# One closing If for the general path, in place of an If between two expert slots and a cascade behind the last

## Chip, cores and metric

The kernel runs on one core of one Trainium2 chip. The metric is the device time of one execution in microseconds (us), median over runs. The core has a matrix engine (TensorE, PE in the profile; its weight loads are PEld), VectorE (DVE), ScalarE (ACT), GpSimd (POOL) and SyncE (SP), which here issues most of the DMAs.

## What is computed

A gated linear attention over 4 x 8 heads, 768 steps, head size 48, then two mixture-of-experts layers (8 experts, one chosen per token, 384 -> 1024 -> 384 with a ReLU), the first with a capacity of 768 tokens per expert, the second with an output gate. There are 3072 tokens, all numbers are float32.

```python
f = 1.0 / (1.0 + np.exp(-f_logit))
for t in range(S):
    state = f[:, :, t, :, None] * state + np.einsum('bhd,bhe->bhde', k[:, :, t], v[:, :, t])
    y[:, :, t] = np.einsum('bhd,bhde->bhe', q[:, :, t], state)
# x: y as [3072, 384]; layer 1
expert_idx = np.argmax(x @ w_gate, axis=1)        # gate_w: its softmax weight
disp[e, counts[e]] = x[i]                         # the first `capacity` tokens of each expert
h = np.maximum(np.einsum('ecd,edf->ecf', disp, w1), 0.0)
y = np.einsum('ecf,efd->ecd', h, w2)
out[i] = gate_w[i] * y[expert_idx[i], pos[i]]     # 0 for a token beyond the capacity
# layer 2: the same with own weights, no capacity, and
out[mask] = gate_w[mask, None] * sigmoid(x @ w_output_gate)[mask, e, None] * ye
```

## The kernel before

**Stages.** `attention` works through 24 blocks of 128 steps; while it does so it routes the tokens of layer 1 (`tok_route`) and scatters their rows, sorted by expert, into a buffer `xs1` in HBM (POOL, L376). Small constants (`iota`, L141 to L157, `consts_late`, L189) are made on the way, one group per block. From about 147 us on the kernel works in *slots*: a slot reads a fixed number of rows of one expert from `xs1`, transposes them (`xt_jobs`, L497), splits them into a high and a low part (xh, xl) and runs both matrix products (`layers`, L1034) with three matmuls for each product: high by high, high by low, low by high. The weights are loaded by SP into `raw` (L218) and split by ACT and DVE (L231, L232) into one of two sets in turn.

**Order of the slots.** The expert with the most tokens is known before attention ends; the first slot, *early*, takes its first 256 rows. Then come the ranks 0 to 7 of layer 1, the experts in order of their counts; rank 0 is the early slot's expert again, with the rest of its rows (112 x 2 = 224) and the same weights. Layer 2 has the same: an early slot and nine slots more (`SLOTS2`). The shapes are fixed at compile time, from 224 to 432 rows.

**What fills the gaps.** `layers` calls `hook(f)` behind each of its eight first-layer tiles (f) and three second-layer tiles (m), and the hooks issue other work there: the routing of the slot before (`post1_jobs`, L1081: matmuls with the gate at L1094, then some 25 small DVE and ACT steps, among them rank matmuls on PE at L329, then scatters into `xs2`), the transposes for the next slot (L503), weight splits, gates. Each engine works through its own instructions in the order in which the program issues them (`manual_schedule`).

**SP's queue around the change.** Row reads (`read_rows`, L1012), zeroing DMAs behind a slot's rows (`rank_zeros` -> `zero_rows`, L210) and weight loads stand in one queue. Reads and zeroing of `xs1` follow one another through the data.

**The general path.** What the fixed slots don't hold is counted in `rare`: a flag of the attention (`fla`, some decay too small), rows beyond the room of the slots (`nover`), rows beyond the capacity (`drop`). For the inputs timed here all are 0 and no part of the general path runs. It stands at two places: between the early slot and rank 0, an If on `rare` (L1267, L1268) that may redo attention and routing and then go through a cascade of eleven nested Ifs (`cascade1`), one leftover slot each; and behind the last slot of layer 2, a second cascade (`cascade2`, L1368) on a count `nv2` (L1364). `plan2.overflow` (L948, 25 DVE operations, in the hooks of the first slot of layer 2) makes that count and the lists for the cascade.

A value is loaded for an If on each engine (`values_load`), and each engine branches by itself. Where the branch skips the body, a few semaphore updates behind it bring the semaphores to the state that the body would have left.

Of the kernel before, what the change touches and what calls it, by code (L numbers as in the profile page):

```python
# [9 lines left out]
F32 = mybir.dt.float32  # L10
F32R = mybir.dt.float32r
# [35 lines left out]
NOV = 11  # L47
# [16 lines left out]
def moe_attention_kernel(ctx: ExitStack, tc, blk, vblk, iw1, iw2, w1a, w2a, w1b, w2b, cap, out):  # L64
# [73 lines left out]

    iota_i = cp.tile([128, E * NOV], I32, name="iota_i")

    def iota(name, shape, pattern, base, cm):  # L141
        ti = iota_i[:, :shape[1]] if len(shape) == 2 else iota_i.rearrange("p (a b) -> p a b", a=shape[1])
# [728 lines left out]
    class Plan:  # L871


        def __init__(self, tag, slots, room, early):
# [10 lines left out]
            self.nf = t("o_nf", [128, 1])  # L885
            self.ni = t("o_ni", [1, 1], I32)
            self.thr = t("o_thr", [128, NOV])
            self.row0 = t("o_row0", [1, NOV], I32)
            self.wrow = t("o_wrow", [1, NOV], I32)
# [58 lines left out]
        def overflow(self):  # L948

            def t(n, shape):  # L950
                if n not in state:
                    state[n] = cp.tile(shape, F32, name=n)
                return state[n]

# [20 lines left out]
            def sm(out, x):  # L975
# [8 lines left out]
                lambda: V.tensor_copy(self.nf, cum[:, E - 1:E]),  # L984
                lambda: V.tensor_copy(self.ni, cum[0:1, E - 1:E]),
# [17 lines left out]
                tt(self.row0, nj[0:1], live[0:1], ALU.mult),  # L1003
                stt(self.wrow, ej[0:1], 128.0, live[0:1], ALU.mult, ALU.mult),
            ]
            return count, where
# [19 lines left out]
    def ovf_rows(xs, o, j):  # L1026
        s = slot(OV, o.thr[:, j:j + 1], xs)
        read_rows(s, xs, o.row0[0:1, j:j + 1])
        return s
# [4 lines left out]
    def layers(s, st, hook, rows_out=False, parts=False):  # L1034
        N = s.N
        hh, hl = ([hbuf[:, i * NM:i * NM + N] for i in range(o, o + KF)] for o in (0, KF))
# [154 lines left out]
    W += [lambda l, j=j: weights_at(plan2.wrow[0:1, j:j + 1], l, wb[l]) for j in range(NOV)]  # L1191
# [15 lines left out]
    wq = ctx.enter_context(tc.tile_pool(name="wq", bufs=1))  # L1207
    whl.append([[wq.tile([128, 3072], F32R, name=f"w{l}{hl}1") for hl in "hl"] for l in (1, 2)])
    hbuf = wq.tile([128, 2 * KF * NM], F32R, name="hbuf")
    wy = ExitStack()  # L1210
    ybuf = [wy.enter_context(tc.tile_pool(name="wy", bufs=1)).tile([128, 2 * KD * NM], F32R, name="ybuf")]

    def outputs(n, parts):

        if not parts and len(ybuf) == 1:
            wy.close()
            ybuf.append(ctx.enter_context(tc.tile_pool(name="wz", bufs=1)).tile([128, KD * NM], F32, name="yT"))
        b = ybuf[0] if parts else ybuf[1]
        return [b[:, i * KD * NM:i * KD * NM + KD * n].rearrange("p (k n) -> p k n", k=KD) for i in range(1 + parts)]
# [28 lines left out]

    def post1_now(s):
        run(gate_jobs(s) + sum(post1_jobs(s), []))  # L1250
        V.tensor_copy(base2, state["base"])
        state["base"] = base2

    def cascade1(j, nv):
        with tc.If(nv > j):
            for l in (0, 1):
                weights_at(plan1.wrow[0:1, j:j + 1], l, wa[l])
            s = ovf_rows(xs1, plan1, j)
            run(xt_jobs(s))
            run(split_jobs(1))  # L1260
            layers(s, 1, lambda i: None, parts=True)
            post1_now(s)
            if j + 1 < NOV:
                cascade1(j + 1, nv)

    at = turn[0]
    rv = nc.values_load(rare[0:1, 0:1], min_val=0, max_val=128 + 2 * E)  # L1267
    with tc.If(rv > 0):  # L1268
        fv = nc.values_load(fli[0:1, 0:1], min_val=0, max_val=128)
        with tc.If(fv > 0):  # L1270
            general_attention()
            reroute()
            state["base"] = base2
            V.memset(early1.offs, 0.0)
            V.memset(early1.thr, 0.0)
            V.tensor_copy(early1.ints[:, 4:5], early1.row[0:1])
            run(plan1.order(base1f, True))
        run(sum(plan1.overflow(), []))
        nc.sync.dma_start(out=out.rearrange("(p j) c -> p j c", j=NT // 128),
                          in_=zrow[:, :DM].unsqueeze(1).to_broadcast([128, NT // 128, DM]))  # L1280
        post1_now(cur)
        V.memset(early1.thr, 0.0)
        for e in range(E):
            zero_rows(xs1, plan1.tail[0:1, e:e + 1], NO)
        cascade1(0, nc.values_load(plan1.ni[0:1, 0:1], min_val=0, max_val=NOV))
        for l in (0, 1):
            W[1](l)
        run(halves(split(1, None, None))[0])
        read_rows(nxt, xs1, early1.ints[0:1, 4:5])
        run(xt_jobs(nxt))  # L1290

    turn[0] = at
# [145 lines left out]
```

## Time and profile before

| | us |
|---|---|
| median of 3 runs | 647.56 (647.36 to 654.54) |
| the profiled execution, its time | 645.49 |
| its span in the trace | 643.7 |
| PE busy | 608.9 (95%) |
| DVE busy | 409.5 (64%) |
| ACT busy | 320.8 (50%) |
| POOL busy | 159.5 (25%) |
| mean granted clock of PE | 0.98 |

The profile is of one execution; its times are those of the trace, counted from the start of the span. A busy share is the share of a stretch in which the engine worked on an instruction; branches, register loads, semaphore updates and the issue of DMAs are not counted as busy. Matmuls are pipelined: a matmul's duration is longer than the distance to the next one's start. The granted clock of PE is in parts of 2.4 GHz.

### The profile page before, as it was taken

Reading aid. Unit: us, or ns where it says so; the run is one execution under the profiler, and the core shown is the slowest. Engines: PE = TensorE matmul, PEld = TensorE weight load, DVE = VectorE, ACT = ScalarE, POOL = GpSimd, SP = SyncE. Lnnn points to the kernel's source line nnn. Section 1 sums busy time; section 2 is a strip of 40 time slices with the busy share of each in tenths; the row PEclk is TensorE's granted clock in tenths of the full one; section 3 lists DMA queues with packets and bytes.
Section 4 is the critical chain, followed back from the end, with each engine's and each line's share of the span. In section 5 each row is a group of like instructions: output and inputs, shape, how many; then the busy total and the mean of one; then the engine's idle time right before and its main releaser. Section 6 shows DMA issues by size and latency. Waiting matters only on the chain.

```text
span 643.7 us, 13335 instructions
## 1 busy us (share of the span) xinstructions
PE 608.9 (95%) x4888; PEld 588.3 (91%) x4888; DVE 409.5 (64%) x1119; ACT 320.8 (50%) x722; POOL 159.5 (25%) x223
## 2 busy tenths in 40 slices
PE   8999998897599999999999999999999999999991
PEld 7898887787599999999999999999999999999991
DVE  7888999978366656657585866618544544654620
ACT  3665654555244453636365463345554544764530
POOL 2567667646001102020202201110110111111120
PEclk9999998999979999999999999999999999999997
DMA  9987884957166446546475272086644435665300
GB/s 237 258 211 205 233 214 140 280 166 280 42 187 217 157 149 177 175 138 198 137 243 170 67 241 76 23 268 193 241 163 135 161 115 189 210 230 150 137 28 21
DMA packets 31540, 110.40 MB, mean 172 GB/s; under 512 B 4109, under 2 KB 15154, under 8 KB 27614
## 3 DMA queue, kind: packets, MB, share of 16 engines
q1 hardware_dynamic: 26158, 95.05, 48.4%
q0 software_dynamic: 5296, 14.30, 6.8%
q8 instruction: 42, 0.69, 0.5%
q14 instruction: 44, 0.36, 0.2%
HBM read 83.47 MB, written 26.21 MB: 170 GB/s over the span
## 4 chain that ended last, share of the span: by engine, by line
PE 40%; issue 26%; POOL 4%; ACT 0%; POOLq 0%
PE pys L1072 17%; PE phs L1044 12%; PE pxs L1044 6%; POOL out L376 4%; PE ptr L1094 1%; PE pys L1094 1%; PE phs L503 1%; PE pxs L503 0%; POOLq L376 0%; ACT w1h L231 0%; ACT hbuf L1046 0%; PE pmt L329 0%; PE pys L1143 0%; PE ptr L1143 0%; ACT yT L1078 0%
## 5 line engine op out<-in xcount | busy, mean ns | idle before, releaser
L1072 PE MATMUL pys<-hbuf,w2h 128*128 128x360 f32 (+10 forms) x864 | 206.8, 321 | 1.0 <-DVE hbuf L1047 1.0
L1072 PEld LDWEIGHTS pys<-hbuf,w2h 128*128 128x128 f32 x864 | 149.8, 188 | 2.5 <-DVE hbuf L1047 1.4
L1072 PE MATMUL pys<-hbuf,w2l 128*128 128x360 f32 (+10 forms) x432 | 137.8, 319 | 0.0
L1044 PE MATMUL phs<-xh,w1h 128*128 128x360 f32 (+10 forms) x306 | 100.9, 330 | 7.0 <-DVEq L1268 4.6
L376 POOL DMA_INDIRECT xs<-xrow,r_dest x53 | 54.9, 1036 | 201.7 <-ACT w2h L231 90.1
L1044 PE MATMUL phs<-xl,w1h 128*128 128x360 f32 (+10 forms) x306 | 98.0, 320 | 0.5 <-DVE xl L505 0.5
L1044 PE MATMUL phs<-xh,w1l 128*128 128x360 f32 (+10 forms) x306 | 97.8, 320 | 0.0
L232 DVE TENSOR_TENSOR w2l<-raw,w2h 128x512 fp32r<-128x512 f32 x96 | 65.5, 686 | 47.0 <-ACT w2h L231 46.5
L232 DVE TENSOR_TENSOR w1l<-raw,w1h 128x512 fp32r<-128x512 f32 x96 | 65.0, 689 | 28.1 <-ACT w1h L231 27.5
L1072 PEld LDWEIGHTS pys<-hbuf,w2l 128*128 128x128 f32 x432 | 81.5, 189 | 0.5
L376 POOL DMA_INDIRECT out<-xrow,oid x31 | 30.2, 975 | 183.8 <-ACT xrow L1144 174.6
L1047 DVE SCALAR_TENSOR_TENSOR hbuf<-phs,hbuf 128x360 fp32r<-128x360 f32 (+10 forms) x102 | 50.9, 499 | 30.8 <-ACT hbuf L1046 30.5
L1046 ACT ACTIVATE hbuf<-phs 128x360 fp32r<-128x360 f32 (+10 forms) x102 | 46.1, 451 | 40.9 <-PE phs L1044 38.8
L1044 PEld LDWEIGHTS phs<-xh,w1h 128*128 128x128 f32 x306 | 58.9, 193 | 7.8 <-issue 4.8
L231 ACT CAST w2h<-raw 128x512 fp32r<-128x512 f32 x96 | 59.2, 622 | 1.3 <-DMA raw<-w2b 1.3
L1044 PEld LDWEIGHTS phs<-xl,w1h 128*128 128x128 f32 x306 | 58.8, 192 | 1.1 <-DVE xl L505 0.7
L1044 PEld LDWEIGHTS phs<-xh,w1l 128*128 128x128 f32 x306 | 59.0, 193 | 0.3
L231 ACT CAST w1h<-raw 128x512 fp32r<-128x512 f32 x96 | 58.0, 621 | 0.0
L1044 PE MATMUL pxs<-xh,w1h 128*128 128x360 f32 (+10 forms) x150 | 49.1, 327 | 0.0
L1075 ACT CAST ybuf<-pys 128x360 fp32r<-128x360 f32 (+5 forms) x27 | 12.3, 454 | 73.3 <-PE pys L1072 71.3
L1078 ACT COPY yT<-pys 128x312 f32<-128x312 f32 (+4 forms) x27 | 11.7, 434 | 73.3 <-PE pys L1072 73.3
L1044 PE MATMUL pxs<-xl,w1h 128*128 128x360 f32 (+10 forms) x150 | 47.9, 320 | 0.0
(262 smaller groups left out, 1076.2 us busy)
## 6 DMA issues: line engine op xcount, KB each, us to landing
fqk<-blk SPq DMA_DIRECT2D x20, 672.0 KB, 7.0
raw<-w1b SPq DMA_DIRECT2D x8, 1536.0 KB, 8.3
raw<-w2b SPq DMA_DIRECT2D x8, 1536.0 KB
raw<-w1a SPq DMA_DIRECT2D x7, 1536.0 KB
raw<-w2a SPq DMA_DIRECT2D x7, 1536.0 KB, 7.8
vt<-vblk SPq DMA_DIRECT2D x24, 256.0 KB, 6.2
xs<-zrow SPq DMA_DIRECT2D x5, 786.0 KB
fqk<-blk SPq DMA_DIRECT2D x12, 224.0 KB, 5.0
```

The costliest lines, as they stand in the source:

```text
L231: A.copy(hi[:, c], raw[l][:, c])
L232: V.tensor_tensor(out=lo[:, c], in0=raw[l][:, c], in1=hi[:, c], op=ALU.subtract)
L376: G.indirect_dma_start(out=dst, out_offset=bass.IndirectOffsetOnAxis(ap=idx, axis=0), in_=src, in_offset=None, bounds_check=bound, oob_is_ ...
L503: PE.transpose(ps[:, j * P:(j + 1) * P], s.xr[:, j, k * 128:(k + 1) * 128], ident[:P, :P])
L1044: PE.matmul(ps, lhsT=w[:, c], rhs=x[:, k], start=(n == 0), stop=(n == 3 * KD - 1))
L1046: A.activation(out=hh[f], in_=ps, func=AF.Relu)
L1047: V.scalar_tensor_tensor(out=hl[f], in0=ps, scalar=0.0, in1=hh[f], op0=ALU.max, op1=ALU.subtract)
L1072: PE.matmul(ps, lhsT=w[:, c], rhs=x, start=(n == 0), stop=(n == 3 * KF - 1))
L1075: A.copy(y[0][:, m], ps)
L1078: A.copy(s.y[:, m], ps)
L1094: PE.matmul(ps[:, k, :w.shape[1]], lhsT=y[:, k, j * P:(j + 1) * P], rhs=w, start=(i == 0), stop=(i == 1))
```

## The change

- The If on `rare` between the early slot and rank 0 goes, with `cascade1`; so does `cascade2` with the load of `nv2`.
- In their place one If stands at the very end, behind the last slot of layer 2. Its condition is again `rare`, which now has the leftovers of layer 2 in it too: the first two counts are added in `count_rare` as before, the third in `plans2`, at the start of layer 2.
- Its body, `again`, does everything anew: it redoes attention and routing if the flag is set, zeroes the output, and then goes through both layers with a loop over `NOV` leftover slots each, where the slot's row and weight indices are shifted by one place per turn (`named`, `next`). `NOV` rises from 11 to 19.
- `plan.overflow` is called in the body alone; its 25 operations leave the first slot of layer 2. Two constants (`ov_m`, `ov_j`) that only it needs are made in the body, and the constants behind them in `consts_late` move up by two blocks of attention.
- The buffers for the second set of weights, h and y are taken from pools that close before the last If.

```diff
-NOV = 11
+
+NOV = (NT + E * (NO - 1)) // NO
...
-    ov_m = iota("ov_m", [128, E, NOV], [[0, E], [NO, NOV]], 0, 0)
     ioe = iota("ioe", [128, E], [[1, E]], 0, 0)
-    ov_j = iota("ov_j", [128, NOV], [[1, NOV]], 0, 0)
...
-        if not parts and len(ybuf) == 1:
+        if ybuf[1] != 1 + parts:
             wy.close()
...
     def count_rare():
         V.tensor_copy(fli, fla[0:1])
         V.tensor_tensor(out=rf, in0=plan1.nover[0:1], in1=plan1.drop[0:1], op=ALU.add)
-        V.tensor_tensor(out=rare, in0=rf, in1=fla[0:1], op=ALU.add)
+        V.tensor_tensor(out=rf, in0=rf, in1=fla[0:1], op=ALU.add)
...
-    def cascade1(j, nv):
-        with tc.If(nv > j):
...
-    at = turn[0]
-    rv = nc.values_load(rare[0:1, 0:1], min_val=0, max_val=128 + 2 * E)
-    with tc.If(rv > 0):
-        fv = nc.values_load(fli[0:1, 0:1], min_val=0, max_val=128)
-        with tc.If(fv > 0):
-            general_attention()
-            reroute()
...
-        cascade1(0, nc.values_load(plan1.ni[0:1, 0:1], min_val=0, max_val=NOV))
...
     def plans2():
         read_rows(nxt, xs2, early2.ints[0:1, 4:5])
         run(plan2.order(state["base"], False))
+        V.tensor_tensor(out=rare, in0=rf, in1=plan2.nover[0:1], op=ALU.add)
...
         if i == 0:
-            lists.append((sum(plan2.overflow(), []), (0, 10)))
             rank_zeros(xs2, plan2, 1)
...
-    nv2 = nc.values_load(plan2.ni[0:1, 0:1], min_val=0, max_val=NOV)
-
-    def cascade2(j, s):
-        n = 2 * E + j
-        with tc.If(nv2 > j):
...
-    cascade2(0, None)
+    def again(more):
+
+        fv = nc.values_load(fli[0:1, 0:1], min_val=0, max_val=128)
+        with tc.If(fv > 0):
+            general_attention()
+            reroute()
+        wr = more.enter_context(tc.tile_pool(name="wr", bufs=1))
...
+        for xs, o, base, capped, src in ((xs1, plan1, base1f, True, wa), (xs2, plan2, base2, False, wb)):
+            V.memset(o.room, 0.0)
+            V.memset(o.early.offs, 0.0)
+            run(o.order(base, capped))
+            o.overflow(wr)
+            for e in range(E):
+                zero_rows(xs, o.tail[0:1, e:e + 1], NO)
+            state["base"] = base2
+            with tc.For_i(0, NOV, 1):
+                o.named()
+                for l in (0, 1):
+                    weights_at(o.at[0:1, 0:1], l, src[l])
+                s = ovf_rows(xs, o)
+                run(xt_jobs(s) + split_jobs(0))
...
+                o.next()
+
+    rv = nc.values_load(rare[0:1, 0:1], min_val=0, max_val=128 + 3 * E)
+    wy.close()
+    late.close()
+    with tc.If(rv > 0), ExitStack() as more:
+        again(more)
```

## Rows read from the trace of the kernel before

**Rows 1.** The page, 40 equal slices: busy tenths of PE.
```profile
PE   8999998897599999999999999999999999999991
```

**Rows 2.** Stretches: from:to, length, busy of PE, PEld, DVE, ACT, POOL (count), clock, DMA.
```profile
165.00:167.00 2.00, 0.93 (x9) 0.93 (x10) 1.47 (x5) 1.14 (x4) 0.00 (x0) 1.00 0.06 23
167.00:169.70 2.70, 2.70 (x24) 2.51 (x22) 0.89 (x3) 0.36 (x2) 0.00 (x0) 1.00 0.03 9
169.70:174.00 4.30, 0.02 (x1) 0.00 (x0) 0.73 (x4) 0.37 (x1) 0.37 (x2) 1.00 0.03 10
174.00:176.00 2.00, 1.64 (x8) 1.67 (x9) 0.00 (x0) 0.00 (x0) 0.00 (x0) 0.52 0.02 4
```

**Rows 3.** The same view of rank 0's slot, up to and from the rank matmuls.
```profile
174.36:185.55 11.19, 11.19 (x58) 11.16 (x58) 3.71 (x14) 3.56 (x9) 0.00 (x0) 0.55 0.45 133
185.55:198.14 12.59, 12.59 (x118) 12.59 (x117) 8.80 (x35) 5.82 (x18) 1.96 (x2) 1.00 0.75 227
```

**Rows 4.** Line 1268: engine's queue, instruction, count: ns min/median/max, first and last start.
```profile
L1268 PEldq COMPARE_BRANCH  x1: 3372/3372/3372, 168.1 to 168.1; - x1
...
L1268 DVEq COMPARE_BRANCH  x1: 72/72/72, 171.3 to 171.3; - x1
...
L1268 DVEq EVENT_SEMAPHORE  x2: 21/21/21, 174.2 to 174.3; - x2
...
L1268 POOLq INC_SWDGE_SEM  x1: 664/664/664, 164.4 to 164.4; - x1
```

**Rows 5.** Timeline of PE: start, us, line, tiles, shape, count [idle before <- ended by].
```profile
166.07 0.41 PE L503 MATMUL pxs<-ident,xrow 112*128 112x112 f32 x2 [1.34 <-DMA xrow<-xs]
...
169.44 0.28 PE L1072 MATMUL pys<-hbuf,w2h 128*128 128x256 f32 x1
174.36 0.53 PE L1044 MATMUL phs<-xh,w1h 128*128 128x224 f32 x1 [4.64 <-DVEq L1268]
...
629.58 0.33 PE L1058 MATMUL pys<-w2h,hbuf 128*112 128x384 f32 x1
```

**Rows 6.** Timeline of DVE ahead of the branch.
```profile
167.21 0.68 DVE L505 TENSOR_TENSOR xl<-phs,xh 128x224 fp32r<-128x224 f32 x2
170.16 0.42 DVE L1076 TENSOR_TENSOR ybuf<-pys,ybuf 128x256 fp32r<-128x256 f32 x1 [2.28 <-ACT ybuf L1075]
```

**Rows 7.** The chain of work that ended last, in order: start, us, what; 182 to 201.
```profile
186.91 2.01 PE phs L1044 x18
...
191.66 0.39 PE pxs L503 x4
...
199.84 0.56 PE ptr L1094 x6
200.40 0.59 PE pys L1094 x6
```

**Rows 8.** Timeline of SP's DMA issues, 160 to 185.
```profile
162.63 0.34 SPq L1012 DMA_DIRECT2D xrow<-xs  x1
175.28 0.64 SPq L210 DMA_DIRECT2D xs<-zrow  x1
180.71 0.40 SPq L1012 DMA_DIRECT2D xrow<-xs  x1
```

**Rows 9.** Line 1368, the closing If of before, and line 1434, the program's end.
```profile
L1368 POOLq EVENT_SEMAPHORE  x4: 17/43/43, 633.7 to 634.0; - x4
...
L1368 POOLq INC_SWDGE_SEM  x1: 1841/1841/1841, 634.1 to 634.1; - x1
...
L1434 POOLq DRAIN  x3: 46/107/6932, 635.9 to 643.4; - x3
```

**Rows 10.** Timeline of POOL in attention, one constant's cast.
```profile
54.01 0.26 POOL L147 CAST ov_m<-iota_i 128x88 f32<-128x88 int32 x1
```

**Rows 11.** A stretch of attention behind a pause of PE, columns as in rows 2.
```profile
106.00:109.00 3.00, 3.00 (x26) 2.39 (x22) 2.84 (x9) 1.59 (x4) 2.54 (x5) 0.50 0.19 70
```

**Rows 12.** Groups of DVE by line, 432 to 449: count, busy us, mean ns, idle before.
```profile
L383 DVE TENSOR_REDUCE o_nkx<-o_ohxb 128x8 f32<-128x64 f32 x1 | 0.3, 277 | 0.0
```

More of the change, by code (lines that the diff above doesn't have):

```diff
@@ L137, in moe_attention_kernel @@
     iotas = []
-    iota_i = cp.tile([128, E * NOV], I32, name="iota_i")
+    iota_i = cp.tile([128, NBLK], I32, name="iota_i")
     def iota(name, shape, pattern, base, cm):
-        ti = iota_i[:, :shape[1]] if len(shape) == 2 else iota_i.rearrange("p (a b) -> p a b", a=shape[1])
+        ti = iota_i[:, :shape[1]]
         tf = cp.tile(shape, F32, name=name)
@@ L946, in order, with overflow, t @@
             return steps
-        def overflow(self):
-            def t(n, shape):
+        def overflow(self, pool):
+            def t(n, shape, dt=F32):
                 if n not in state:
-                    state[n] = cp.tile(shape, F32, name=n)
+                    state[n] = pool.tile(shape, dt, name=n)
                 return state[n]
+            ov_i, ov_m, ov_j = t("ov_i", [128, E, NOV], I32), t("ov_m", [128, E, NOV]), t("ov_j", [128, NOV])
+            G.iota(ov_i, pattern=[[0, E], [NO, NOV]], base=0, channel_multiplier=0)
+            G.tensor_copy(ov_m, ov_i)
+            G.iota(ov_i[:, 0], pattern=[[1, NOV]], base=0, channel_multiplier=0)
+            G.tensor_copy(ov_j, ov_i[:, 0])
+            self.thr, self.turn = t("o_thr", [128, NOV]), t("o_turn", [128, NOV])
+            self.row0, self.wrow = t("o_row0", [128, NOV]), t("o_wrow", [128, NOV])
+            self.at = t("o_at", [1, 2], I32)
             def over_e(x):
@@ L1002, in overflow, with named, next @@
                 stt(nj, ej, float(R), nj, ALU.mult, ALU.add),
-                tt(self.row0, nj[0:1], live[0:1], ALU.mult),
-                stt(self.wrow, ej[0:1], 128.0, live[0:1], ALU.mult, ALU.mult),
-            ]
-            return count, where
+                tt(self.row0, nj, live, ALU.mult),
+                stt(self.wrow, ej, 128.0, live, ALU.mult, ALU.mult),
+            ]
+            run(count + where)
+        def named(self):
+            for i, t in enumerate((self.wrow, self.row0)):
+                V.tensor_copy(self.at[:, i:i + 1], t[0:1, 0:1])
+        def next(self):
+            for t in (self.thr, self.row0, self.wrow):
+                V.tensor_copy(self.turn, t)
+                V.tensor_copy(t[:, :NOV - 1], self.turn[:, 1:])
     plan1, plan2 = Plan("a", SLOTS1, room[0], early1), Plan("b", SLOTS2, room[1], early2)
@@ L1024, in rank_zeros, with ovf_rows @@
             zero_rows(xs, o.behind[0:1, r:r + 1], n)
-    def ovf_rows(xs, o, j):
-        s = slot(OV, o.thr[:, j:j + 1], xs)
-        read_rows(s, xs, o.row0[0:1, j:j + 1])
+    def ovf_rows(xs, o):
+        s = slot(OV, o.thr[:, 0:1], xs)
+        read_rows(s, xs, o.at[0:1, 1:2])
         return s
@@ L1035, in layers @@
         N = s.N
-        hh, hl = ([hbuf[:, i * NM:i * NM + N] for i in range(o, o + KF)] for o in (0, KF))
+        hh, hl = ([hbuf[0][:, i * NM:i * NM + N] for i in range(o, o + KF)] for o in (0, KF))
         (w1h, w1l), (w2h, w2l) = whl[st]
@@ L1387, in moe_attention_kernel @@
-    cascade2(0, None)
+    def again(more):
[4 more added lines that the diff above has]
+        wr = more.enter_context(tc.tile_pool(name="wr", bufs=1))
+        hbuf[0] = wr.tile([128, 2 * KF * NM], F32R, name="hbuf")
+        ybuf[:] = wr.tile([128, 2 * KD * NM], F32R, name="ybuf"), 2
+        nc.sync.dma_start(out=out.rearrange("(p j) c -> p j c", j=NT // 128),
+                          in_=zrow[:, :DM].unsqueeze(1).to_broadcast([128, NT // 128, DM]))
+        V.tensor_copy(base2, base0)
+        for xs, o, base, capped, src in ((xs1, plan1, base1f, True, wa), (xs2, plan2, base2, False, wb)):
[8 more added lines that the diff above has]
+                o.named()
+                for l in (0, 1):
+                    weights_at(o.at[0:1, 0:1], l, src[l])
+                s = ovf_rows(xs, o)
+                run(xt_jobs(s) + split_jobs(0))
+                if capped:
+                    layers(s, 0, lambda i: None, parts=True)
+                    run(gate_jobs(s) + sum(post1_jobs(s), []))
+                    V.tensor_copy(base2, state["base"])
+                    state["base"] = base2
+                else:
+                    post2_jobs(s)
+                    s.ids()
+                    layers(s, 0, lambda i: None, True)
+                o.next()
```

70 lines of the change are left out of this document (8 added, 62 removed).

## Prediction

> **What bounds the kernel now.** Read TensorE's (PE's) busy shares by slice first [rows 1]. The expert slots begin in the tenth slice of 16 us; from the twelfth (177 us) to the last but one PE is at nine tenths or more, and the dip to five just before is the slice with the first If. So the slots are bound by PE, and each microsecond there in which PE doesn't work, or not at full clock, is one of the total. What DVE, ACT, POOL or SP lose or gain counts only where PE ends up waiting for them.
>
> Next PE's timeline [rows 5]: the last matmul of the early slot starts at 169.44, the first of rank 0 at 174.36, after 4.64 us of idling that DVE's queue at L1268 ended, the line of `tc.If(rv > 0)`.
>
> Then the stretches around it [rows 2]. The granted clock is 1.00 (2.4 GHz) up to 174, also in 165 to 167, where PE was busy only 0.93 of 2 us; in 174 to 176 it is 0.52, nearly all at the lower level, 1.2 GHz. [Rows 3] give what follows: from 174.36 to 185.55 the mean is 0.55 with PE busy throughout, from 185.55 on 1.00. So the If costs PE twice: a pause, and half clock behind it.
>
> Why the pause: every engine takes the branch over the body for itself, and its first instruction behind it comes late [rows 4]. PE's compare-and-branch lasts 3.37 us from 168.1, so to 171.5, 2 us after PE has run out of matmuls. DVE branches later, at 171.3, for it first owes the early slot's output [rows 6]; its first instruction behind the branch, a semaphore update that stands for the skipped work, is at 174.2. That one releases PE.
>
> **The change part by part, against the profiled execution (645.49 us, span 643.7).**
>
> 1. The If between the early slot and rank 0 goes: five loads of `rare`, five taken branches, the updates. PE goes from the early slot's last matmul into rank 0's first, at 169.44 + 0.11 (24 of these matmuls in 2.70 us, [rows 2]) = 169.55 instead of 174.36: **4.8 us**. What else could be late there? xh and xl come from DVE at L505, two instructions in the 0.68 us from 167.21, so done at 167.9 [rows 6]; the weights are those that the early slot has just used. Behind nine matmuls PE needs ybuf (L1094), at 169.55 + 1.01 = 170.56; it is written at 170.16 + 0.42 = 170.58. So nothing holds PE by more than a tenth.
>
> 2. The half clock behind the pause. From 174.36 to the rank matmuls at 185.55 PE does 45 matmuls of L1044 with 224 columns (five tiles of nine) and 12 of L1094 ([rows 3] count 58, one over the edge). At full clock 18 of L1044 take 2.01 us, 0.112 each, and in the next slot 12 of L1094 take 0.56 + 0.59 = 1.15 [rows 7]. 45 x 0.112 + 1.15 = 6.2 us against 11.19: **5.0 us**, if the clock stays at 1.00.
>
> 3. What is late next: at full clock rank 0's first tiles want DVE and ACT sooner. They are busy 3.71 and 3.56 us in that stretch [rows 3], which must now fit in 6.2. Both fit, but as chains: the router's one-hot must be there when the fifth tile ends, and behind each PSUM tile stand a Relu on ACT, a subtraction on DVE, router steps and weight splits. From 185.55 on DVE does 8.80 us in 12.59 with PE busy throughout. I give back **0.5 us**, between 0 (all hidden) and 1.0 (one tile of nine matmuls spent waiting).
>
> 4. SP loses its wait at the If. The zeroing DMA behind rank 1 goes out at 175.28, rank 1's row read at 180.71, rank 0's read went at 162.63 [rows 8]. They are chained through the same buffer in HBM: zeros when rank 0's rows have landed, at 166.1, where PE transposes them [rows 5]; then the read, 5.4 us behind as now, at 171.5. PE transposes rank 1's rows at 191.66 [rows 7], 9.3 us earlier after the change, 182.4. With 3.5 us for the landing (162.63 to 166.1) 7.4 are left over. Rank 2's weights, queued behind these on SP, come earlier by as much. Worth 0; without this cover a late read would hold PE for at most its 3.5.
>
> 5. The planner of leftovers (`plan2.overflow`, 8 + 17 DVE operations in the first slot of layer 2) goes; one addition for `rare` comes. The longest of the 25 takes 0.28 us [rows 12], so at most 7 us of DVE in all, beside a PE that is at nine tenths or more there [rows 1] and waits for none of them: 0.
>
> 6. Constants in the attention stage: two iotas and their casts go from POOL (0.26 us for the larger cast, [rows 10]); room, gate and split constants come two blocks earlier. A change of order can matter there: behind a pause of PE the clock is at 0.50 from 106 to 109 [rows 11]. Such a dip could vanish or a second arise: 3 us at half clock are 1.5 of work. I take 0, bounds 1.5 either way.
>
> 7. The closing If. One stands there now (L1368) and one after, with one load, one branch and updates per engine. The end hangs on POOL [rows 9]: first update behind the branch 633.7, a software-DMA semaphore update of 1.84, a drain of 6.93. Same order, same steps: 0. The body skipped then has loops in it, but so has the one at L1268, and there each engine went through its own updates as it arrived [rows 4]. Bounds: 1.2 less (that update took 0.66 at L1268) and 2.9 more (one more fetch in the chain, DVE's 171.3 to 174.2).
>
> Sum: 645.49 - 4.8 - 5.0 + 0.5 = 636.2. The median of the runs, 647.56, is 2.07 above the profiled execution; carried over: **638.2 us**, 1.4% faster.
>
> A rule against the first term: the Trainium skill, "Advanced Engine Details and Errata", section Control Flow Timing, gives about 108 ns for a compare-and-branch; by it term 1 would be some 0.1 us, no clock would be lost to it, and the time would be about 647. The trace has 3372 ns for it on PE, so the row decides. The skill's "Runtime: NRT & Kernel Launch", section Instruction fetch mechanics, has a taken branch wait for its target to be fetched where that isn't held; with that the trace agrees, and it would leave the closing branch at its price.
>
> **Rivals.**
> A. As summed: 638.2, by the bounds of 3, 6 and 7 from 636 to 641. Chance 0.77.
> B. The pause goes and the clock falls all the same: PE has gaps from 165 to 167, just before. Against it: 1.00 up to 174. Gain 4.8 alone: 642.8. Chance 0.08.
> C. It isn't the branch: the releaser shown is only the last of several, and PE waits at that place for something else as long, or a new stall takes back what was won (a late read, 3.5, and a clock drop behind it, 5.0). 647.6, or 646.7. For it would speak a branch that costs next to nothing; against it, that each producer named under 1 is done by 170.6. Chance 0.05.
> D. The other side: the closing If becomes dearer. If its updates make the engines wait for one another in turn, five fetches stand in a row in place of one: four more of 2.9 us are 11.6, and 638.2 + 11.6 = 649.8, slower than before. It decides once more than three fetches are added (9.3 / 2.9 = 3.2). For it: both layers, loops and all engines are now in one body. Against: at L1268 they ran side by side. Chance 0.05.
> E. More than summed: the dip at 106 goes (1.5), the update at the end is short (1.2), nothing is given back (0.5): 635.0, or with a little more under 634.6. Chance 0.05.
>
> **How the numbers follow.** The predicted time is A's. A and B hold 0.85; 635.5 to 643.0 takes them in with their bounds and leaves out C, D and E. Two per cent of 647.56, about what a measurement of this kernel can tell from no change, are 13 us: faster means below 634.6, most of E, 0.04; slower means above 660.5, D with as much again on top, 0.01; within 2%: 0.95.
>
> **What would show it.** Right, if PE has no wait at all on an If's line before the closing one, and none over 1 us between the early slot and rank 0; if the clock is 1.00 from 165 through rank 0; if rank 0's first tile starts near 169.6 and its rank matmuls come 6 to 7.5 us later; if PE's last matmul starts near 620.3 (now 629.58, [rows 5]) with some 14 us behind it. Wrong, if the clock shows 0.50 behind 170 (B), if PE's waits have a new row at L1044, L1094 or L503 (C), or if much more than 14 us follow PE's last matmul (D).

## The result: 637.46 us, 1.3% less

| | before | after |
|---|---|---|
| median of 6 runs each (lowest to highest) | 647.68 (644.50 to 654.54) | 637.46 (635.06 to 642.32) |
| profiled execution | 645.49 | 635.73 |
| its span in the trace | 643.7 | 634.0 |

The ratio of the medians is 0.9866, 95% interval 0.9821 to 0.9911: a gain of 1.3%, with an interval that lies below 1. The forecast was 638.2, in 635.5 to 643.0.

Lines have moved: the first weight product (L1044 before) is now L1055, the second (L1072) L1083, the router product (L1094) L1105, the row transposes (L503) L502, the rank matmuls L328, the layer 2 product with which PE ends (L1058) L1069, and the closing If (L1368) L1372.

The profile of the kernel after, first its page: busy tenths of PE and its granted clock, in 40 slices.

```profile
PE   8999998998899999999999999999999999999990
...
PEclk9899998989999999999999999999999999999996
```

The five in the eleventh slice of [rows 1] is now an eight. What stands there shows in the same stretches as [rows 2 and 3] (from:to, length, busy of PE, PEld, DVE, ACT, POOL, granted clock, DMA):

```profile
165.00:167.00 2.00, 1.68 (x15) 1.68 (x16) 1.87 (x7) 1.26 (x4) 0.19 (x1) 1.00 0.21 78
167.00:169.70 2.70, 2.70 (x26) 2.70 (x25) 0.61 (x3) 0.37 (x1) 0.00 (x0) 1.00 0.74 247
169.70:174.00 4.30, 4.30 (x41) 4.30 (x40) 2.67 (x15) 2.63 (x6) 0.00 (x0) 1.00 0.42 110
174.00:176.00 2.00, 2.00 (x22) 1.97 (x22) 1.89 (x6) 1.36 (x5) 0.00 (x0) 1.00 0.36 91
168.81:175.17 6.36, 6.36 (x60) 6.33 (x58) 4.13 (x18) 3.76 (x9) 0.00 (x0) 1.00 0.41 106
175.17:187.76 12.59, 12.59 (x118) 12.55 (x117) 8.83 (x36) 5.88 (x18) 1.95 (x2) 1.00 0.77 225
```

The third line was 0.02 us of PE in 4.30 and is now 4.30. The fifth is rank 0 up to its rank matmuls: 6.36 us at full clock where [rows 3] had 11.19 at 0.55. The sixth, the 12.59 us behind, has 118 matmuls at full clock in both.

PE's timeline (start, us, line, tiles, shape, count) has the seam and the end:

```profile
165.32 0.41 PE L502 MATMUL pxs<-ident,xrow 112*128 112x112 f32 x2 [0.83 <-DMA xrow<-xs]
...
168.69 0.28 PE L1083 MATMUL pys<-hbuf,w2h 128*128 128x256 f32 x1
168.81 0.27 PE L1055 MATMUL pxs<-xh,w1h 128*128 128x224 f32 x1
...
175.17 0.20 PE L328 MATMUL pmt<-r_oh,ones 128*128 128x16 bf16 x2
...
619.29 0.33 PE L1069 MATMUL pys<-w2h,hbuf 128*112 128x384 f32 x1
```

Rank 0's first matmul follows the early slot's last by 0.12 us. In [rows 5] it was 4.92 (169.44 to 174.36). PE's list of waits (engine, line, releaser: us in total, times, longest) names no If, and nothing at the seam. The row at L1055 belongs to the early slot's start; in the kernel before, the same 2.0 us stood at L1044:

```profile
PE phs L631 <- POOL kh L623: 5.0, 6, 1.8
PE phs L1055 <- DVE xl L504: 2.0, 2, 1.4
...
PE pxs L502 <- DMA xrow<-xs: 0.8, 1, 0.8
```

Behind PE's last matmul the end goes on as in [rows 9]. The closing If, line 1372 (queue, instruction, count: ns min/median/max, first and last start), and line 1420, the program's end:

```profile
L1372 POOLq EVENT_SEMAPHORE  x6: 17/30/355, 623.5 to 624.3; - x6
...
L1372 PEldq COMPARE_BRANCH  x1: 3857/3857/3857, 616.9 to 616.9; - x1
...
L1372 POOLq COMPARE_BRANCH  x1: 57/57/57, 620.9 to 620.9; - x1
L1372 POOLq INC_SWDGE_SEM  x1: 1856/1856/1856, 624.4 to 624.4; - x1
```

```profile
L1420 POOLq DRAIN  x3: 46/107/6937, 626.3 to 633.7; - x3
```

Read in these four marks, the two traces give the whole difference:

| stretch of the span | before | after | difference |
|---|---|---|---|
| start to the early slot's last matmul (attention in it) | 169.44 | 168.69 | -0.75 |
| from there to rank 0's first matmul | 4.92 | 0.12 | -4.80 |
| from there to the rank matmuls | 11.19 | 6.36 | -4.83 |
| from there to PE's last matmul | 444.03 | 444.12 | +0.09 |
| from there to the end of the span | 14.12 | 14.71 | +0.59 |
| span | 643.7 | 634.0 | -9.70 |

The seam gives 9.63 of the 9.70 us. Neither the first row nor the last is clear of what moves between two executions of one kernel, as the last table of the experiments tells.

### The profile page after: what moved, and what is told of

Same layout as the page of the kernel before. It is cut to its first block, busy times and chain, and to the rows that moved or that the text cites. A ratio compares the mean times of both kernels' runs of the same rounds, so it can differ in the third digit from the quotient of the medians.

```text
span 634.0 us, 13249 instructions
## 1 busy us (share of the span) xinstructions
PE 606.6 (96%) x4888; PEld 586.6 (93%) x4888; DVE 405.2 (64%) x1095; ACT 320.7 (51%) x722; POOL 157.8 (25%) x219
## 4 chain that ended last, share of the span: by engine, by line
PE 54%; issue 30%; POOL 7%; DVE 4%; DMA 2%; ACT 1%; POOLq 0%; DVEq 0%; SPq 0%; ACTq 0%
PE pys L1083 18%; PE phs L1055 12%; PE pxs L1055 6%; POOL out L375 4%; PE phs L631 3%; PE ptr L654 3%; PE ptr L669 2%; DMA fqk<-blk 2%; PE ptr L687 2%; PE pys L635 2%; PE ptr L1105 1%; POOL kh L623 1%; PE pys L1105 1%; DVE Pt L606 1%; PE phs L502 1%
## 5 line engine op out<-in xcount | busy, mean ns | idle before, releaser
L1083 PE MATMUL pys<-hbuf,w2h 128*128 128x360 f32 (+10 forms) x864 | 206.9, 322 | 0.9 <-DVE hbuf L1058 0.6
L1083 PEld LDWEIGHTS pys<-hbuf,w2h 128*128 128x128 f32 x864 | 149.8, 188 | 2.4 <-DVE hbuf L1058 0.8
L1083 PE MATMUL pys<-hbuf,w2l 128*128 128x360 f32 (+10 forms) x432 | 137.8, 319 | 0.0
L1055 PE MATMUL phs<-xh,w1h 128*128 128x312 f32 (+10 forms) x306 | 99.4, 325 | 2.3 <-DVE xl L504 1.4
L1055 PE MATMUL phs<-xl,w1h 128*128 128x312 f32 (+10 forms) x306 | 96.9, 317 | 0.5 <-DVE xl L504 0.5
L1055 PE MATMUL phs<-xh,w1l 128*128 128x312 f32 (+10 forms) x306 | 96.7, 316 | 0.0
L1083 PEld LDWEIGHTS pys<-hbuf,w2l 128*128 128x128 f32 x432 | 81.5, 189 | 0.5
L1058 DVE SCALAR_TENSOR_TENSOR hbuf<-phs,hbuf 128x312 fp32r<-128x312 f32 (+10 forms) x102 | 50.7, 498 | 23.9 <-ACT hbuf L1057 23.2
L1057 ACT ACTIVATE hbuf<-phs 128x312 fp32r<-128x312 f32 (+10 forms) x102 | 46.1, 452 | 33.8 <-PE phs L1055 33.0
L1055 PEld LDWEIGHTS phs<-xh,w1h 128*128 128x128 f32 x306 | 57.7, 188 | 3.1 <-DVE xl L504 1.7
L1055 PEld LDWEIGHTS phs<-xl,w1h 128*128 128x128 f32 x306 | 57.7, 189 | 1.1 <-DVE xl L504 0.7
L1055 PEld LDWEIGHTS phs<-xh,w1l 128*128 128x128 f32 x306 | 57.8, 189 | 0.3
L1089 ACT COPY ybuf<-pys 128x312 f32<-128x312 f32 (+4 forms) x27 | 11.7, 434 | 73.5 <-PE pys L1083 73.5
L1055 PE MATMUL pxs<-xh,w1h 128*128 128x360 f32 (+10 forms) x150 | 48.8, 325 | 0.0
L1055 PE MATMUL pxs<-xl,w1h 128*128 128x360 f32 (+10 forms) x150 | 47.6, 318 | 0.0
```

The source lines that it names most:

```text
L1055: PE.matmul(ps, lhsT=w[:, c], rhs=x[:, k], start=(n == 0), stop=(n == 3 * KD - 1))
L1057: A.activation(out=hh[f], in_=ps, func=AF.Relu)
L1058: V.scalar_tensor_tensor(out=hl[f], in0=ps, scalar=0.0, in1=hh[f], op0=ALU.max, op1=ALU.subtract)
L1083: PE.matmul(ps, lhsT=w[:, c], rhs=x, start=(n == 0), stop=(n == 3 * KF - 1))
```

## Experiments

The theory: the branch over a far body stopped PE for 4.8 us, the stop then cost it the full clock for 5.0, and nothing else that the change does reaches PE or the end. Rivals: the place itself held PE, or other edits made the gain; the clock falls because of the branch or of what it fetches, not of the stop; the closing If is what changed. Each ratio is to runs of the kernel before on the same chip: both Ifs at the seam, the pause of 5 and the kernel without a closing If share one set (median 647.25, 19 runs); the kernel before without its If, the stand-ins and the repeats another (648.72, 13 runs); the pause of 1 and the other two closing Ifs a third (651.84, 3 runs).

**1. The If put back, with a far and with a near target.** Both start from the kernel after and put an If of the same condition as before's at the seam. The far one has attention's general path in its body, the near one a single memset.

```diff
+        V.tensor_copy(rare1, rf)
...
     state["base"] = base2
+    rv1 = nc.values_load(rare1[0:1, 0:1], min_val=0, max_val=128 + 2 * E)
+    with tc.If(rv1 > 0):
+        general_attention()
```

In the near one the last line is `V.memset(scr, 0.0)`.

> The kernel after, with an If on the counts of layer 1 put back between the early slot and rank 0; its body is the general attention alone (long, never entered here; for inputs with a nonzero count the output would not be the reference's). Theory (far branch: a pause on PE, then half clock): PE idles 4.6 to 5.0 us ahead of rank 0's first matmul, the granted clock is 0.50 to 0.60 from there to the rank matmuls, which come 11 us behind the first matmul instead of 6.4; time about 637.5 + 9.6 = 647. Rival (the gain came from elsewhere: constants of the attention, the planner, the closing If): 641 or less.

Measured: 649.47 us, ratio to before 1.0020 (0.9975 to 1.0065): the whole gain is gone. PE's timeline, the stretches around the seam (columns as above) and the If's line:

```profile
178.30 0.53 PE L1055 MATMUL pxs<-xh,w1h 128*128 128x224 f32 x1 [4.66 <-DVEq L1264]
```

```profile
175.00:177.00 2.00, 0.00 (x0) 0.00 (x0) 0.00 (x0) 0.00 (x0) 0.00 (x0) 0.64 0.07 12
177.00:179.00 2.00, 0.70 (x3) 0.73 (x4) 0.00 (x0) 0.00 (x0) 0.00 (x0) 0.50 0.42 68
179.00:186.00 7.00, 7.00 (x36) 7.00 (x35) 1.68 (x7) 2.38 (x5) 0.00 (x0) 0.52 0.56 190
186.00:190.00 4.00, 4.00 (x41) 3.98 (x40) 3.15 (x11) 1.90 (x8) 0.00 (x0) 1.00 1.06 246
```

```profile
L1264 PEldq COMPARE_BRANCH  x1: 5249/5249/5249, 172.0 to 172.0; - x1
...
L1264 DVEq COMPARE_BRANCH  x1: 72/72/72, 175.2 to 175.2; - x1
...
L1264 DVEq EVENT_SEMAPHORE  x1: 21/21/21, 178.1 to 178.1; - x1
```

The pause is [rows 5]' own, 4.66 us of idling released from DVE's queue, and half clock follows it as in [rows 3]. DVE's first update stands 2.9 us behind its branch, as in [rows 4] (171.3 to 174.2).

> The same If at the same place, its body one memset of DVE, so that the branch goes only a few instructions ahead (the body is never entered here; the general path for it stays at the end). Theory (it is the late first instruction behind a far branch): each engine goes on at once behind its branch, DVE's update comes 0.7 us (load 0.54, branch 0.07) behind its last work, PE waits about 2 us, the clock stays 1.00; time 637.5 + 2 = 639.5. Rival (any If costs it, by the loads of the condition and the updates in turn): a pause of 4.6 or more, half clock behind it, 647.

Measured: 641.67 us, ratio 0.9872 (0.9822 to 0.9921). The same line of this kernel:

```profile
L1264 PEldq COMPARE_BRANCH  x1: 228/228/228, 173.5 to 173.5; - x1
...
L1264 DVEq COMPARE_BRANCH  x1: 72/72/72, 176.2 to 176.2; - x1
L1264 DVEq EVENT_SEMAPHORE  x1: 21/21/21, 176.5 to 176.5; - x1
```

PE's branch takes 228 ns in place of 5249, and DVE's update comes 0.3 us behind its branch in place of 2.9; DVE has one such update in both. So an If at this place is nearly free as long as its target is near, and it is the way to a far one that costs. The 2 us of waiting that were expected did not come: rank 0's first matmul follows at 0.12 us, for PE's first nine don't need what DVE owes behind its branch, and only DVE waited, 0.7 us. One later slot of this execution was 1.0 us longer (27.90 for 26.9); why stays open.

What DVE waited for can be seen in part. In the 2.9 us from its branch to its first update the far If's trace has three DMA packets of the kind "instruction" (queue and kind: packets, MB, share of 16 engines):

```profile
q14 instruction: 2, 0.02, 2.9%
q8 instruction: 1, 0.02, 2.1%
```

Both traces of the kernel before have the same three between DVE's branch and its first update; the near If has none in the 2.9 us from its branch. So instructions are fetched there, though the trace doesn't say which packet is for which engine. And not every engine pays at every If: ACT goes on 0.4 us behind its branch in the far one (174.5 to 174.9).

**2. The stop without an If.** DVE gets work ahead of rank 0's first operand, so that PE stops as long as it did at the If, but no engine branches. `scr` holds zeros. The short pause has `range(1)` in place of `range(5)`.

```diff
     state["base"] = base2
+    for _ in range(5):
+        V.tensor_tensor(out=scr, in0=scr, in1=scr, op=ALU.add)
+    V.tensor_tensor(out=nxt.xl[:, 0], in0=nxt.xl[:, 0], in1=scr[:, :nxt.N], op=ALU.add)
```

> The kernel after, no If in the middle; on DVE five additions of 128x512 on a scratch tile (0.69 us each) and then one that rewrites xl of rank 0 with zeros added, between the early slot and rank 0. PE does two matmuls and then waits for xl, some 4.8 us. Theory (the clock falls because PE stands still, whatever holds it): granted clock 0.50 behind the pause for about 10 us as behind the If; 637.5 + 4.8 + 4.8 = 647. Rival (the clock falls only with the branch, by its fetch or its semaphores): clock 1.00, 637.5 + 4.8 = 642.

Measured: 649.64 us, ratio 1.0017 (0.9982 to 1.0052). PE's timeline and stretches:

```profile
180.48 0.55 PE L1055 MATMUL pxs<-xl,w1h 128*128 128x224 f32 x1 [4.97 <-DVE xl L1264]
```

```profile
177.00:179.00 2.00, 0.00 (x0) 0.00 (x0) 1.90 (x4) 0.00 (x0) 0.00 (x0) 1.00 0.47 91
179.00:181.00 2.00, 0.52 (x2) 0.52 (x3) 1.36 (x3) 0.00 (x0) 0.00 (x0) 0.50 0.73 220
...
187.00:189.00 2.00, 2.00 (x12) 2.00 (x11) 1.59 (x6) 0.94 (x3) 0.00 (x0) 0.50 1.01 246
189.00:191.00 2.00, 2.00 (x22) 1.98 (x21) 0.87 (x3) 1.04 (x4) 0.00 (x0) 0.94 0.89 362
```

Rank 0 up to its rank matmuls takes 15.75 us from its first matmul, which starts before the stop: 6.36 of the kernel after, 5.0 of stop, and 4.4 that are left for the lower clock, here 0.50 from 179 to 189. So the clock needs no branch to fall; a stop of this length does it, and with it the time of the kernel before is there again.

> As pause5 with one addition in place of five: PE waits some 2 us for xl of rank 0, no If in the middle. Theory (as from 165 to 167 in the kernel before, where PE worked 0.93 of 2 us and the clock stayed): clock 1.00 throughout, 6.4 + 2.1 = 8.5 us from rank 0's first matmul to the rank matmuls. Rival (the clock falls behind any stop at this place, since PE has gaps from 163 on): 0.50 behind it, 12 to 13 us.

Measured: 642.32 us in 2 runs, ratio 0.9875 (0.9738 to 1.0012). The interval reaches above 1, so what follows rests on the trace.

```profile
172.00 0.37 PE L1055 MATMUL pxs<-xl,w1h 128*128 128x224 f32 x1 [2.07 <-DVE xl L1264]
```

```profile
171.00:173.00 2.00, 1.00 (x9) 1.00 (x9) 0.91 (x2) 0.00 (x0) 0.00 (x0) 1.00 0.31 53
173.00:175.00 2.00, 2.00 (x14) 2.00 (x13) 0.90 (x5) 0.94 (x2) 0.00 (x0) 0.64 0.79 226
175.00:177.00 2.00, 2.00 (x11) 2.00 (x11) 0.23 (x1) 0.58 (x1) 0.00 (x0) 0.50 0.27 55
177.00:179.00 2.00, 2.00 (x20) 2.00 (x20) 1.49 (x6) 1.23 (x3) 0.00 (x0) 1.00 0.41 155
```

Neither expectation held. The theory had the clock stay at 1.00, and it fell; the rival had it cost as much as behind the long stop, and it was at 1.00 again from 177. The stretch took 10.31 us: 6.36, 2.07 of stop, and 1.9 for the clock. So a stop of less than half the length was paid twice too, in proportion.

**3. The kernel before without its If at the seam.** If other edits had a share in the gain, the kernel before would still be slower than after.

```diff
-    rv = nc.values_load(rare[0:1, 0:1], min_val=0, max_val=128 + 2 * E)
-    with tc.If(rv > 0):
-        ...
```

> The kernel before without the If between the early slot and rank 0 and its cascade (that part of the general path is left out); second cascade, planner and constants as before. Theory (that If is all of it): no pause, 6.4 us to the rank matmuls, 444.1 on, 14.1 to the end: 9.7 less than before_2 by the trace, 638 by time. Rival (planner, constants and closing If have a share): gain under 8.5 by the trace, or over 11.

Measured: 639.50 us, ratio 0.9851 (0.9804 to 0.9897), beside 638.54 us, 0.9825 (0.9796 to 0.9854), for the kernel after on the same chip. Rank 0 from its first matmul to just short of the rank matmuls' end, stretch columns as above:

```profile
172.16:178.64 6.48, 6.48 (x61) 6.46 (x59) 4.13 (x18) 3.76 (x9) 0.00 (x0) 1.00 0.44 106
```

Counted from its own first matmul at 172.28 it is 6.36 us at full clock, as in the kernel after. The two stretches at the seam (last table) are 9.48 us shorter than in the second trace of before, of 10.1 by which the span is shorter; the rest lies in stretches that move from execution to execution. So this If alone is the gain, as far as these runs can tell (639.50 and 638.54 are within the spread of the runs, 637.42 to 642.78 here), and nothing else held PE at this place.

**4. The closing If: without it, with a near target, and with its updates ahead of the jump.** All three start from the kernel after. The first takes the If out, with its load:

```diff
-    rv = nc.values_load(rare[0:1, 0:1], min_val=0, max_val=128 + 3 * E)
...
-    with tc.If(rv > 0), ExitStack() as more:
-        again(more)
```

> The kernel after without the closing If and its load: the general path is left out. Theory (the end is a chain on POOL: branch, late first instruction, updates, then a drain of fixed length): from PE's last matmul to the end 14.7 - 5 = about 10 us, POOL's drain again 6.9, starting right behind the last scatter; time 633. Rival (the drain waits for what POOL's last scatter still does, so the If is hidden under it): the drain is longer, 14 us or so behind the last matmul, 637.

Measured: 636.63 us, ratio 0.9815 (0.9771 to 0.9860). In the trace 10.19 us follow PE's last matmul (623.51) in place of 14.71. The program's end:

```profile
L1417 POOLq DRAIN  x3: 46/107/8113, 624.6 to 633.2; - x3
```

The drains begin 1.1 us behind PE's last matmul where those of the kernel after begin 7.0 behind it (626.3 less 619.29), 5.9 sooner; the long one then takes 8.11 us in place of 6.94. It now begins while POOL's last scatter is still to come:

```profile
624.79 0.94 POOL L375 DMA_INDIRECT out<-xrow,oid  x1 [3.24 <-ACT xrow L1135]
```

That scatter ends at 625.73, and the long drain at 632.67, 6.94 later. So the drain's length is the one expected, counted from the end of the scatter; the 1.2 us that it begins too soon are given back, and the end gains 4.5 where 5 were expected. The time expected, 633, wasn't reached: up to the early slot's last matmul this execution took 172.73 us, the first one of the kernel after 168.69.

The second leaves load and If and puts a memset in the body:

```diff
-    with tc.If(rv > 0), ExitStack() as more:
-        again(more)
+    with tc.If(rv > 0):
+        V.memset(scr, 0.0)
```

> The kernel after with one memset of DVE as the body of the closing If (the general path is left out). Theory (the closing If costs POOL's far branch and the updates of the skipped scatters): the end comes 10.2 + 0.6 (load and branch on POOL) = 10.8 us behind PE's last matmul, POOL goes on within 0.3 us of its branch. Rival (any closing If costs it): 14.7.

Measured: 631.17 us in 2 runs, ratio 0.9703 (0.9582 to 0.9825); 10.03 us follow PE's last matmul (619.07). The closing If and the program's end in this kernel:

```profile
L1373 PEldq COMPARE_BRANCH  x1: 223/223/223, 616.7 to 616.7; - x1
...
L1373 POOLq COMPARE_BRANCH  x1: 57/57/57, 620.7 to 620.7; - x1
```

```profile
L1421 POOLq DRAIN  x3: 46/113/7363, 620.9 to 628.8; - x3
```

The If and its load are still there, and cost nothing that the end shows: POOL goes from its branch at 620.7 into the drains at 620.9, still ahead of the end of its last scatter (621.28), and the long drain again ends 6.94 us behind that. So the 0.6 us added for load and branch were hidden. That the time is less than without any closing If is no gain of this one: the early slot ended at 168.38 in this execution and at 172.73 in that. In the kernel after 5.4 us lie between these two (620.9 to 626.3): 2.6 to the first update behind the branch, 0.9 of updates, 1.86 of the software-DMA update. So it is the far target and the updates for the skipped work that cost the closing If its 4.5 us.

The third keeps all of it, and is an attempt at a kernel that beats both: each engine is to fall through into the updates and to jump only behind them.

```diff
-    with tc.If(rv > 0), ExitStack() as more:
+    with tc.If(rv > 0, preferred_fallthrough_block=False), ExitStack() as more:
         again(more)
```

> The kernel after, the closing If laid out so that the updates for the skipped body stand right behind the branch and a jump over the body follows them; nothing is left out. Theory (the jump's target comes late as the branch's did, the order alone changes): 14.5 us behind PE's last matmul, within 0.5. Rival (the updates, above all POOL's 1.86, run while something else is waited for): 13 or less.

Measured: 640.65 us in 2 runs, ratio 0.9849 (0.9725 to 0.9973); 16.83 us follow PE's last matmul, 2.1 more than in the kernel after. The closing If:

```profile
L1372 POOLq EVENT_SEMAPHORE  x6: 17/30/2363, 623.1 to 625.8; - x6
...
L1372 POOLq COMPARE_BRANCH  x2: 41/42/43, 623.0 to 627.8; - x2
L1372 POOLq INC_SWDGE_SEM  x1: 1856/1856/1856, 625.9 to 625.9; - x1
```

Theory and rival were both wrong on this one. The updates do begin right behind POOL's first branch (623.0 to 623.1), but one of them now lasts 2.36 us, the software-DMA update has its 1.86 as before, and only then, at 627.8, comes the jump to the far target that POOL still has to make. The way there is paid behind the updates in place of ahead of them, and a wait is added. That wait is likely one for POOL's last scatter to land, though no run tests it: it ends 3.1 us behind the scatter's start at 622.65. In the kernel after, the longest update (0.36 us) ends 3.6 us behind the start of the same scatter, which took 3.6 us to land there, so all but 0.36 of the wait passed while POOL stood at its branch. The attempt failed.

**5. The planner put back as stand-ins.** 25 operations of 128x88 on DVE in the first slot of layer 2, where `plan2.overflow` was, and the two constants on POOL at their old place.

```diff
+            lists.append(([lambda: V.tensor_tensor(out=scr, in0=scr, in1=scr, op=ALU.add)] * 25, (0, 10)))
             rank_zeros(xs2, plan2, 1)
...
+    ov_m = iota("ov_m0", [128, 88], [[1, 88]], 0, 0)
     ioe = iota("ioe", [128, E], [[1, E]], 0, 0)
+    ov_j = iota("ov_j0", [128, 11], [[1, 11]], 0, 0)
```

> The kernel after with 25 DVE operations of 128x88 in the hooks of the first slot of layer 2, and with two iotas and casts at their old places in attention. Theory (all hidden): 444.1 us from rank matmuls to PE's last matmul, as in after_2, time within 0.5% of after_2. Rival (DVE's steps delay PE in that slot): 445 to 449 there.

Measured: 640.49 us, ratio 0.9848 (0.9812 to 0.9885). The slot with the stand-ins takes 22.23 us from its first matmul to that of the next slot; in the kernel after on the same chip it is 21.42, and in the kernel before on the same chip, with the real planner, 21.42 too. The stretch from the rank matmuls to PE's last matmul is 444.94, at the rival's edge. A stretch of 4 us in that slot, first with the stand-ins, then in the second trace of before, each with PE's share first and DVE's third:

```profile
434.00:438.00 4.00, 3.91 (x27) 3.53 (x26) 3.86 (x13) 2.45 (x7) 0.00 (x0) 1.00 0.39 104
```

```profile
443.00:447.00 4.00, 4.00 (x30) 4.00 (x30) 3.93 (x13) 2.82 (x6) 0.00 (x0) 1.00 0.41 108
```

The real planner was hidden, with DVE full to 3.93 of 4 us and PE not waiting. The stand-ins (25 at 247 ns) no longer are, and cost 0.81; they are more work than the planner was: in this slot DVE is busy 17.34 us with them, 15.72 with the planner and 13.18 with neither. So the planner's removal is worth nothing in this kernel, but with 1.6 us more of DVE work it would no longer have been hidden.

**6. Both kernels once more, unchanged, in the second set.**

> The kernel before once more, for a second profile on the same chip as the other runs of this set. Theory (attention's end moves from execution to execution, the slots don't): pause 4.9 us start to start, 11.2 from rank 0's first matmul to the rank matmuls, 444.0 from there to PE's last matmul, 14.1 to the end, each within 0.3; only the start of rank 0 (174.4 in the first profile) may be elsewhere. Rival (the slots vary too): 444.0 is off by over 1.

> The kernel after once more, same set. Theory: no pause, 6.4 us to the rank matmuls, 444.1 on, 14.7 to the end, whatever the start of rank 0 (168.8 in the first profile, 172.9 to 175.1 in other variants with the same attention). Rival (the change itself moves attention): rank 0 starts 0.5 to 1 us earlier than before_2's pause begins, as in the first pair of profiles (168.81 against 169.55).

Measured: 649.38 us (0.9994, 0.9973 to 1.0016) and 638.54 us (0.9825, 0.9796 to 0.9854). The slots came as expected in both. Rank 0's start did not answer the rival: it came 2.4 us ahead of the start of the pause in before, outside its 0.5 to 1, and later in other kernels with the attention of after. The two traces answer what was left of the first row of the difference, attention. The same marks in PE's timeline of all traces; attention is the same code within a few constants in them (us):

| kernel | early slot's last matmul | from it to rank 0's first | from there to the rank matmuls | to PE's last matmul | to the end |
|---|---|---|---|---|---|
| before | 169.44 | 4.92 | 11.19 | 444.03 | 14.12 |
| before, again | 173.76 | 4.98 | 10.98 | 444.06 | 14.32 |
| far If | 173.37 | 4.93 | 10.00 | 444.15 | 14.45 |
| before without the If | 172.16 | 0.12 | 6.36 | 444.44 | 14.92 |
| after | 168.69 | 0.12 | 6.36 | 444.12 | 14.71 |
| after, again | 171.31 | 0.12 | 6.36 | 444.13 | 14.58 |
| near If | 174.35 | 0.12 | 6.51 | 445.16 | 14.76 |
| stand-ins | 174.45 | 0.12 | 6.36 | 444.94 | 14.63 |
| pause of 5 | 175.01 | 0.12 | 15.75 | 444.25 | 14.67 |
| pause of 1 | 169.44 | 0.12 | 10.31 | 444.39 | 14.64 |
| no closing If | 172.73 | 0.12 | 6.36 | 444.30 | 10.19 |
| closing If near | 168.38 | 0.12 | 6.36 | 444.21 | 10.03 |
| updates ahead of the jump | 170.77 | 0.12 | 6.36 | 444.13 | 16.83 |

From the rank matmuls on the slots repeat within some tenths, but for the near If and the stand-ins with one longer slot each. The first column moves by 4.3 us between two executions of before and by 2.6 between two of after. Not all of that is attention: of the 4.3 us, 2.7 lie ahead of the early slot's first matmul (146.52 and 149.21), and 1.6 in the early slot, where the second execution was at half clock for a while and the first wasn't (columns as above):

```profile
150.72:157.54 6.82, 6.24 (x31) 5.85 (x32) 3.57 (x12) 1.45 (x5) 3.70 (x5) 0.50 0.81 248
```

So the 0.75 us of the first pair can't be put down to the change, and whether the constants that moved do something in attention stays open. The end moves too, 14.12 to 14.92 us with the closing If of before and 14.45 to 14.76 with that of after, so its +0.59 isn't clear of the spread either.

## Why the prediction came out right, step by step

- **What bounds the kernel**: PE does, in the slots. Every microsecond that the If cost PE came off the span, and no other engine took one back.
- **Term 1, the pause**: 4.8 expected, 4.80 measured. The cause is shown by the far If, which brings back 4.66 us of idling with the same releaser, and by the near one, which brings back none. "The target is far", argued from [rows 4], is shown by 5249 against 228 ns on PE and 2.9 against 0.3 us behind DVE's branch. The Trainium skill, "Runtime: NRT & Kernel Launch", section Instruction fetch mechanics, says that a taken branch to a target not in the fetched window waits for a fetch; these runs agree, with three instruction packets behind the far branch and none behind the near one. About 108 ns for a compare-and-branch, as the Trainium skill, "Advanced Engine Details and Errata", section Control Flow Timing, has it, is the size of the branch's own record with a near target (72 ns on DVE, 57 on POOL, 228 on PE); with a far one the records of DVE and POOL are the same and the wait stands behind them. Rank 0's operands were in time. One of them the prediction read wrongly: xh comes from ACT (L504), not from DVE; it was done by 167.36, so nothing hangs on it.
- **Term 2, the clock**: 5.0 expected, 4.83 measured; the clock is 1.00 from 165 to PE's last matmul. That the stop makes it fall, and not the branch, was an assumption at the time; the pause of DVE work shows it. The price isn't a constant: for the same stop of about 4.9 us it was 4.83, 4.62 and 3.64 (11.19, 10.98 and 10.00 less 6.36). The lower level itself lasted 10.2 us in all three (174.1 to 184.3, 178.0 to 188.3, 175.5 to 185.8); what differs is how much of it fell into the stop, where half clock costs nothing. With the far If that was 2.8 us (columns as above):

```profile
175.54:178.30 2.76, 0.00 (x0) 0.03 (x1) 0.00 (x0) 0.00 (x0) 0.00 (x0) 0.50 0.13 26
```

  PE worked in the remaining 10.0, 9.5 and 7.5 us, and half of these is 5.0, 4.8 and 3.7, near what was lost. The pause of DVE work fits too: 8.8 of its 10.2 us, so 4.4.
- **Term 3, the give-back**: 0.5 taken, within 0 to 1.0; it was 0. PE is busy for all 6.36 us, with DVE at 4.13 and ACT at 3.76. The chain that came nearest is the router's one-hot, here in DVE's timeline:

```profile
174.71 0.17 DVE L314 TENSOR_TENSOR r_oh<-dec,r_vx 128x16 bf16<-128x16 f32 x1
```

  It ends at 174.88, 0.3 us before the rank matmuls at 175.17 read it. This is the term that was mis-sized, on the safe side.
- **Term 4, SP**: 0, and it was 0. SP's timeline has the two issues close to where they were worked out (166.1 and 171.5), and rank 1's transposes came at 181.17 without a wait:

```profile
165.29 0.62 SPq L209 DMA_DIRECT2D xs<-zrow  x1
170.91 0.38 SPq L1023 DMA_DIRECT2D xrow<-xs  x1
```

- **Term 5, the planner**: 0, and it was 0 (21.42 us for the slot with and without it). The reason given, a PE that waits for none of it, held, but only just; "at most 7 us of DVE" in one slot was not a safe amount.
- **Term 6, attention**: 0 within 1.5 either way; -0.75 in this pair, and that it lay within the bounds is luck. They were too narrow: they were made from one dip in one trace [rows 11], while the stretch up to the early slot's last matmul ends up to 4.3 us apart from execution to execution of the same code.
- **Term 7, the closing If**: 0, within -1.2 and +2.9; +0.59. The order of [rows 9] stayed: branch, updates, software-DMA update of 1.86 us, drain of 6.94. "Same steps" isn't quite so: POOL has six updates where [rows 9] have four, one of them of 0.36 us, and the load of the condition takes 501 ns where it took 306. These make up the 0.59, which isn't more than the end moves by itself. Engines went through their updates side by side, and rival D's five fetches in a row did not come.
- **Rivals**: A's 636 to 641 is narrower than the bounds that it names, which together reach from 635.0 to 643.1; the stated range is close to that. B fell with the clock at 1.00 throughout. C fell with the kernel before less its If. E's larger gain did not come.
- **The marks**: rank 0's first tile at 168.81 (near 169.6 expected), 6.36 us to the rank matmuls (6 to 7.5), PE's last matmul at 619.29 (620.3) with 14.71 behind it (some 14). The profiled execution was worked out at 636.2 and took 635.73: the misses of terms 3, 6, 7 and 2 and of the slots partly cancel (-0.5, -0.75, +0.59, +0.2, +0.1), and the rest of -0.1 lies outside the span. So that it came within half a microsecond is partly luck; the two terms that make the gain were each within 0.2.

## What to carry to other kernels

An If that is never taken cost little here as long as its body was short. If the body to be jumped over is long, engines pay for the way to the far target (here 2.6 us on POOL, 2.9 on DVE, 3.4 to 5.2 on PE), and an engine can be held further by another's updates behind it. Put such a body where the bottleneck engine has no work behind it, which here is the program's end. A stop of the bottleneck engine PE, of 2 or 5 us, was paid up to twice, once as idling and once in half clock behind it, so a pause in the trace is to be read together with the clock of the next ten microseconds. Where a change takes a stop away, look for what is late next in chains of the newly compressed stretch; here they had 0.3 us to spare.

## What the runs showed of the hardware that was not expected

- A stop of 2.07 us in the slots was enough for half clock behind it (0.64 in 173 to 175, 0.50 in 175 to 177), and it was over sooner than behind 4.97 us (0.50 until 189). In the kernel before the clock had stayed at 1.00 with PE busy 0.93 of 2 us in smaller pieces [rows 2].
- Updates for skipped work that are put ahead of the jump made the end 2.1 us longer, with one update of 2.36 us on POOL, likely a wait for the last scatter to land.
- The long drain of POOL at the program's end takes 6.93 to 6.99 us in all 13 traces, if it is counted from its start or from the end of POOL's last scatter, whichever is later. It is longer by its own record in the two kernels in which it begins ahead of the scatter's end (7.36 begun 1.8 us behind PE's last matmul, 8.11 begun 1.1 behind; the scatter ends 2.2 behind it). So what POOL does until then costs the end nothing.
- The closing If still costs 4.5 us (14.71 against 10.19 and 10.03 behind PE's last matmul). Whether it can be had with the general path kept stays open; the one attempt made the end longer.
